# Turning h by DMA instead of on TensorE, and spreading the forward convolution over three blocks of the down product

## The chip, the cores and the metric

The kernel runs on one core of a Trainium2 chip. Its time is the device time of one execution in microseconds (us). In profiles the engines are called PE (TensorE, the matrix engine), PEld (its weight loads), DVE (VectorE), ACT (ScalarE), POOL (GpSimd) and SP (SyncE, which here only issues DMAs). A letter q behind an engine's name (SPq) means the engine's queue, where instructions wait and DMAs are issued.

## The reference

One call computes a small model's output and the gradients of all its inputs but one. S is 2048 rows, D is 1024, F is 3584; all tensors are bf16.

```
xn = layernorm(q)
kv = (4-tap shift convolution of k) * v
y  = causal convolution of kv with ssm_k over the rows (by FFT) + kv * ssm_D
s  = xn * y
h  = (xn @ w_gate) * (xn @ w_up)          # [S, F]
g  = silu(h @ w_down)                     # [S, D]
out = q + s * g
# outputs: out, then the gradients of sum(out * grad_out)
# by q, k, v, shift_k, ssm_k, ssm_D, w_gate, w_up, w_down
```

## The kernel before

The work runs in stages, each with its own matmuls on PE; the long convolution and its gradient run beside them, on DVE mostly.

1. **Start** (to 64 us): layer norm, transposes of xn (tiles `XNT`), tables for the Fourier transforms.
2. **Gate/up** (64 to 518 us): for 14 slabs `sl` of 256 columns of F and 16 row blocks, `gu_unit` multiplies four row blocks (a unit: 32 matmuls of 512 columns, line 645) with the slab `wslab`. ACT copies the products from PSUM to `gut` (647), DVE multiplies the two halves into `hN` (659), POOL stores `hN` to `Hd` (660) for the backward pass. The down product needs h with F on the partitions, so a function `turn` transposes each unit's eight 128x128 blocks on PE into PSUM (674); ACT copies them to `hT` (675); SP stores `hT` to the DRAM tensor `HTd` (666). `turn` is not called at once: `defer` puts it in a list, and `flush(5)` in each tick of a later unit calls the entries that are old enough.
3. **Down product, forward** (518 to 718 us): 16 blocks of 128 rows, 28 steps `fc` over F with two matmuls each (`bm_mm`, 969). The first two blocks run together in `bm_first`. `ht` tiles hold h turned, loaded from `HTd`; `WD` holds w_down, in seven loads. PSUM holds three blocks. Each finished block goes through `gate` (ACT: `bm`, `sig`, `sgn`; DVE: 11 multiplications and additions; POOL: four stores; SP: four loads, among them `yf_t`, the convolution's result, which `YFd` holds).
4. The gradients: dh and the gradients of w_gate and w_up (718 to 1335 us), of w_down (to 1523 us), of xn with the layer norm (to the end).

The **forward convolution** is a generator, `conv_forward`. For each of eight column blocks `ds` it transforms kv (`psF<-kv` on PE, ACT copies `SP`, sums on DVE into `W`, `KX`, `HX`), transforms the filter (`psF<-hx`), multiplies the spectra (`product`), and goes back (`inv_dft` on DVE, then `psY` on PE and `yf` on ACT, in `tail`). Every second `ds` computes the next kv (`shift`). `tick` pulls the generator: after `cnt` ticks it has to have done a share of its estimated work that `NT` sets. DVE's order is the order in which the operations are pulled (`PIN`, `keep_in_program_order`); the order on the other queues is a scheduler's. `drain` pulls what is left. In the kernel before, `bm_first` ticks 0.74 at every second step from step 5 on, and the generator is drained behind `bm_first`, before the gates of the first two blocks. At the end of the gate/up stage the flag `forward` is asserted to be down: the last `product` has begun, and the PSUM pool `ps_cv` of the transforms is given back.

Pools that matter here: `hN` has three buffers, `hT` two, `wslab` two, `ps_y` (PSUM of `psY`) one. The gates' pools (`mi`, `mt`, `mo`) take the room that the convolution's pools leave.

Of the kernel before, what the change touches and what calls it, by code (L numbers as in the profile page):

```python
# [19 lines left out]
def build_kernel(  # L20
# [11 lines left out]
    nc = tc.nc  # L32
# [579 lines left out]
    later = []  # L612
    gu_mm = [None]

    def defer(fn):
        later.append([0, fn])

    def flush(age=0):

# [8 lines left out]

    def gu_unit(sl, b0, n, w, tick):

        if n == 4:
            turn_of[0] += 1
            if turn_of[0] % 3 == 0 and sl < NSL - 2:
                gut = U[5][:, 2048:4096].rearrange("p (a i f) -> p a i f", a=2, i=4)
            else:
                gut = fg.tile([P, 2, 4, SLW], BF16, name="gut")
            hN = fg.tile([P, 2, 4, P], BF16, name="hN", bufs=3)
        else:
            gut = lnp.tile([P, 2, 2, SLW], BF16, name="gut_s", bufs=6)
            hN = lnp.tile([P, 2, 2, P], BF16, name="hN_s", bufs=6)  # L640
        for i in range(n):
            q, qi = divmod(b0 + i, 4)
            ps = ps_gu.tile([P, 512], F32, name="psg")
            for dc in range(DC):
                gu_mm[0] = nc.tensor.matmul(ps[:], XNT[q][:, dc, qi * P:(qi + 1) * P],  # L645
                                            w[:, dc].rearrange("p a f -> p (a f)"), start=(dc == 0), stop=(dc == DC - 1))
            nc.scalar.copy(out=gut[:, :, i], in_=ps[:].rearrange("p (a f) -> p a f", a=2))  # L647
            flush(5)
            if i == 0:
                turn_late()  # L650
            hn[0]()
            hn[0] = nop
            tick()
        sta(GUd[sl, b0 // 8][:, :, b0 % 8:b0 % 8 + n], gut[:, :, 0:n])

        def multiply():
            with tc.issue_after(last.ins) if b0 + n <= 4 and chunk[0] <= 2 else nullcontext():
                by_half = lambda t: t.rearrange("p i (a f) -> p a i f", a=2)
                tt(hN[:, :, 0:n], by_half(gut[:, 0, 0:n]), by_half(gut[:, 1, 0:n]), MUL)
            st(Hd[sl][:, :, b0:b0 + n, :], hN[:, :, 0:n])  # L660
            defer(turn)
        hn[0] = multiply

        def store(hT):
            fr, so = sl % 12 * SLW, b0 % 8 * P
            ld(HTd[b0 // 8][sl // 12][fr:fr + SLW, so:so + n * P].rearrange("(a f) s -> f a s", f=P),
               hT[:, :, 0:n].rearrange("f a i s -> f a (i s)"))

        def turn():
            hT = fg.tile([P, 2, 4, P], BF16, name="hT") if chunk[0] > 5 else lnp.tile([P, 2, 4, P], BF16, name="hT_s", bufs=5)  # L670
            ps = ps_tr.tile([P, 2, 4, P], BF16, name="tr")
            for a in range(2):
                for i in range(n):
                    nc.tensor.transpose(ps[:, a, i, :], hN[:, a, i, :], ident[:])
            nc.scalar.copy(out=hT[:, :, 0:n], in_=ps[:, :, 0:n])
            store(hT)
# [3 lines left out]
    INV8 = (2, 4, 6)  # L680
    SHIFT_W = 8 * 2.3

    conv_state = {"forward": True}

    def conv_forward():
        S_ = conv_state
# [83 lines left out]

        def transform(ds, kind, sp, X, C, ahead, step):

            if (ds, kind) in EIGHT:
                W = fwd4_buf(cs)[:].rearrange("p a b c x -> p (a b c) x")
                for n, w in enumerate(fwd8(sp, X, W, C, ahead)):
                    if n in (0, 2, 4, 6):
                        step()
                    yield net(w)
                return
            W = fwd4_buf(cs)  # L780
            fwd4_sums(W, sp[0], 0)
            step()
            yield net(2.4)
            fwd4_sums(W, sp[1], 1)
            step()
            yield net(2.4)
            fwd4_outs(X, W, 0)
            ahead(0)
            step()
            yield net(2.4)  # L790
            fwd4_outs(X, W, 1)
            ahead(1)
            step()
            yield net(2.4)
# [9 lines left out]
        for ds in range(8):  # L804
            yield 0.5
            if ds % 2 == 1 and ds < 7:
                with tc.issue_after(S_["kst"].ins):
                    for c in range(2):
                        load_kv(ds // 2 + 1, c)
            D0 = Dz[:, ds * P:(ds + 1) * P]  # L810
            sph = []
            KX = cx.tile([P, 16, 256], BF16, name="KX")
            HX = cs.tile([P, 16, 256], BF16, name="HX", bufs=2)
            own_room = lambda X: X[:].rearrange("p a x -> p (a x)").bitcast(F32).rearrange("p (a x) -> p a x", a=8)[:, 0:4]
            eight = (ds, 1) in EIGHT
            if ds == 0:
                yield from transform(0, 1, sp, HX, own_room(KX), lambda i: sph.append(half(0, kvs(0), i)), nop)
            else:
                yield from transform(ds, 0, sp, KX, own_room(HX), lambda i: sph.append(half(ds, S_["hx"], i, D0)), nop)
                S_["kst"] = st(KFd[ds], KX[:])  # L820
            next(tl, None)
            room = cf.tile([P, 4, 256], F32, name="room", tag="hx")[:] if eight else None
            yield from transform(ds, int(ds > 0), sph, HX if ds else KX, room, nop1 if eight else lambda c: h_rows(ds + 1, c),
                                 lambda: next(tl, None))
            if ds == 0:
                S_["kst"] = st(KFd[0], KX[:])
            if eight:
                h_rows(ds + 1, 0)
            turned(HX, 1, 0, 1)
            yield 1.3  # L830
            if eight:
                h_rows(ds + 1, 1)
            if ds == 7:
                cf.release()
                S_["forward"] = False
            st(HFd[ds], HX[:])
            yield from product(KX, HX, KX, cs, False, 0)
            if ds % 2 == 1 and ds < 7:
                yield from shift(ds // 2 + 1)
            sp = []  # L840

            def ahead():
                if ds < 7:
                    sp.append(half(ds + 1, kvs(ds + 1), len(sp)))
            yield from (inv8 if ds in INV8 else inv_dft)(KX, HX, cs, ahead if ds % 2 == 0 else None, ahead)
            if ds % 2 == 1:
                ahead()
            S_["G", ds] = HX
            tl = tail(ds)
# [61 lines left out]
    ps_cv = pool("ps_cv", 2, space=PSUM)  # L911
    pump, drain = make_pump(conv, F_TOTAL)
    cnt = [-5]
    NT = 24 * 8.0 + 14

    def tick(by=1):
        cnt[0] += by
# [55 lines left out]
    def bm_first(fcs):  # L973
        for fc in fcs:
            for i in range(2):
                mm = bm_mm(pss[i], lambda fc: HT0[fc // 16][:, fc % 16], i, fc)
            if fc % 2 == 1 and fc > 4:
                tick(0.74)
        return mm

    assert not conv_state["forward"]
    ps_cv.release()
    ps_bm = pool("ps_bm", 2, side="right", space=PSUM)
    pss = [ps_bm.tile([P, D], F32, name="psbm") for i in range(2)]
    with tc.issue_after(bm_first(range(4)).ins):
        flush()
    for p_ in (ps_gu, fg, fw):
        p_.release()

    ub = pool("ub", 1, side="right")
    U += [ub.tile([P, 4096], BF16, name=f"U{i}") for i in range(8, 12)]
    bw = pool("bw", 2, side="right")
    mh = [pool("mh0", 1, side="right")]
    ps_bx = pool("ps_bx", 1, space=PSUM)
# [181 lines left out]
    bpump, bdrain = make_pump(conv_backward(), C_TOTAL)  # L1179

    ddo = const.tile([P, 8], BF16, name="ddo")
    WD += [u8(j, a=4) for j in (2, 3, 9)]
    DBMT = [u8(q, a=DC) for q in (10, 8, 4, 5)]

    tr_name = ["tr"]
# [44 lines left out]
        return wdt  # L1230

    def load_ht(bp):
        if bp == 1:
            two_ = [u8(10, a=16), u8(8, a=16)]
            for f0, f1 in ((0, 16), (16, 24), (24, 28)):
                last = ld(two_[f0 // 16][:, f0 % 16:f0 % 16 + f1 - f0], ht_rows(bp, f0, f1))
            return (lambda fc: two_[fc // 16][:, fc % 16]), last
        ht = mh[bp % 2].tile([P, NF, 256], BF16, name="ht")
        for f0, f1 in ((0, 24), (24, 28)):
            last = ld(ht[:, f0:f1], ht_rows(bp, f0, f1))  # L1240
# [8 lines left out]
            ld(t, GUd[k // 2, k % 2])  # L1249
            DGU[k] = t  # L1250

    for j in range(4, 7):
        wd_ld = load_wd(j)
    with tc.issue_after(wd_ld.ins):
        ht1 = load_ht(1)
    with tc.issue_after(ht1[1].ins):
        ht2 = load_ht(2)
    bm_first(range(4, NF))
    drain()
    PIN[0] = False  # L1260
    mh.append(pool("mh1", 1, side="right"))
    mi = pool("mi", 2, side="right")
    mt = pool("mt", 1, side="right")
    mo = pool("mo", 2, side="right")
    for i in range(2):
        gate(i, pss[i])
    for bp in range(1, 8):
        ht, ht_ld = load_ht(bp) if bp > 2 else (ht1, ht2)[bp - 1]
        if bp in (3, 5, 7):
# [7 lines left out]
        for i in range(2):  # L1277
            ps = (ps_bx if (2 * bp + i) % 3 == 2 else ps_bm).tile([P, D], F32, name="psbm")
            for fc in range(NF):
                bm_mm(ps, ht, i, fc)  # L1280
                if fc == 18:
                    flush()
            gate(2 * bp + i, ps)
    for p_ in (ps_bx, ps_tr, ps_y, ps_bm, mo, mt, mi, mh[1], mh[0]):
        p_.release()
# [346 lines left out]
```

## Time and profile before

Median of three runs: 1928.6 us (1928.4 to 1930.85). The profiled execution took 1929.26 us; its span, from the first to the last instruction, is 1927.5 us. TensorE's granted clock was 1.00.

| stage (us) | PE busy | DVE busy | ACT busy | DMA share |
|---|---|---|---|---|
| 0 to 64 | 57.65 | 56.30 | 41.68 | 0.91 |
| 64 to 518 | 448.54 | 447.15 | 257.27 | 0.72 |
| 518 to 559 | 40.98 | 13.79 | 10.16 | 0.81 |
| 559 to 718 | 159.00 | 102.74 | 44.60 | 0.98 |
| 718 to 1335 | 616.88 | 547.65 | 185.38 | 0.74 |
| 1335 to 1523 | 188.00 | 143.07 | 40.21 | 0.86 |
| 1523 to 1927.5 | 400.88 | 231.84 | 59.35 | 0.87 |

The columns are busy time in us in each stretch; the DMA share is the mean busy share of the core's 16 DMA engines. A line such as `L674 PE MATMUL tr<-ident,hN 128*128 128x128 bf16 x416 | 31.9, 219 | 1.7 <-DVE hN L213 1.7` is a group of instructions: source line, engine, operation, what it writes from what, shape, count; then busy us in total and mean ns of one; then idle us of the engine just before them, and who ended it. DVE operations all have line 213, that of a helper, so they are told apart by their tiles. Matmuls overlap, so the time that one takes from PE's stream is read from the distance between starts: 0.216 us for 512 columns.

### The profile page before, as it was taken

The page shows a single profiled execution, that of the slowest core. Times are in us where ns is not written, and L with a number is a line of the kernel's source. Part 1 is how long each engine was busy: PE and PEld are TensorE (multiplying, and loading weights), DVE is VectorE, ACT ScalarE, POOL GpSimd, SP SyncE. Part 2 cuts the span into 40 slices and gives each one's busy share as a digit, 9 for nine tenths or more (in the row PEclk, how much of TensorE's full clock was granted, in tenths as well). Part 3 has the DMA queues.
Part 4 walks back from the last instruction along what each step waited for, and adds up shares of the span by engine and source line. Part 5 has one row for each costly group of instructions (what it writes and reads, how often), then busy time and mean ns, then how long its engine had stood idle before and what let it go on. Part 6 is the DMA issues. An engine that isn't in the chain of part 4 may idle for free.

```text
span 1927.5 us, 27456 instructions
## 1 busy us (share of the span) xinstructions
PE 1911.9 (99%) x10978; PEld 1030.1 (53%) x10978; DVE 1542.5 (80%) x1695; ACT 638.7 (33%) x943; POOL 331.0 (17%) x461
## 2 busy tenths in 40 slices
PE   8999999999999999999999999999999999999999
PEld 5555555555444456665666666664444444444444
DVE  8999999999937555888899999999996404287884
ACT  5854555555432233343222322222222102011113
POOL 5121212111112210000122131021211101011111
PEclk9999999999999999999999999999999999999999
DMA  9776866758899987666788698575786999889975
GB/s 297 264 259 221 257 211 229 234 197 266 270 278 312 298 291 257 209 201 218 264 243 264 234 247 263 201 262 186 224 253 174 143 205 217 168 178 188 189 180 171
DMA packets 451360, 444.43 MB, mean 231 GB/s; under 512 B 268800, under 2 KB 371612, under 8 KB 436768
## 3 DMA queue, kind: packets, MB, share of 16 engines
q1 hardware_dynamic: 394848, 243.36, 47.9%
q0 software_dynamic: 40064, 169.95, 27.6%
q10 hardware_dynamic: 16320, 29.36, 4.2%
q8 instruction: 86, 1.41, 0.3%
q14 instruction: 42, 0.34, 0.1%
HBM read 194.00 MB, written 185.64 MB: 197 GB/s over the span
## 4 chain that ended last, share of the span: by engine, by line
PE 80%; DVE 15%; issue 3%; DMA 1%; ACT 1%; SPq 0%; POOL 0%; DVEq 0%; ACTq 0%; POOLq 0%
PE psb L1340 20%; PE psx L1470 20%; PE psb L1323 10%; PE psbm L969 10%; PE psb L1418 9%; PE psg L645 6%; DVE W L213 4%; DVE KX L213 3%; DVE HX L213 2%; DVE m L213 2%; PE psF L235 1%; DVE U L213 1%; DVE hN L213 1%; PE psY L438 1%; PE psY L1116 1%
## 5 line engine op out<-in xcount | busy, mean ns | idle before, releaser
L645 PE MATMUL psg<-wslab,U 128*128 128x512 bf16 x1792 | 407.2, 379 | 2.5 <-DMA wslab<-in_B_w_gate_dram 1.6
L1340 PE MATMUL psb<-U,U 128*128 128x512 bf16 x1792 | 397.1, 379 | 0.0
L1470 PE MATMUL psx<-U,dgut 128*128 128x512 bf16 x1536 | 332.8, 379 | 0.0
L1470 PEld LDWEIGHTS <-dgut 128*128 128x128 bf16 x1792 | 175.3, 98 | 211.4
L1340 PEld LDWEIGHTS <-U 128*128 128x128 bf16 x1792 | 175.2, 98 | 198.0
L645 PEld LDWEIGHTS <-U 128*128 128x128 bf16 x1792 | 172.5, 98 | 187.7 <-issue 2.3
L1323 PE MATMUL psb<-wdt,U 128*128 128x256 bf16 x1792 | 205.6, 273 | 0.0
L1323 PEld LDWEIGHTS <-U 128*128 128x128 bf16 x1792 | 175.3, 98 | 29.2
L1418 PE MATMUL psb<-U,U 128*128 128x512 bf16 x816 | 177.1, 379 | 0.0
L213 DVE TENSOR_TENSOR W<-W 128x1024 f32<-128x1024 f32 (+1 forms) x174 | 171.6, 1003 | 3.7
L1345 ACT CAST wb<-psb 128x512 bf16<-128x512 f32 x112 | 65.6, 586 | 315.1 <-PE psb L1340 313.4
L969 PE MATMUL psbm<-U,ht 128*128 128x512 bf16 x672 | 145.7, 379 | 0.0
L1418 PEld LDWEIGHTS <-U 128*128 128x128 bf16 x896 | 87.5, 98 | 104.5
L647 ACT CAST gut<-psg 128x512 bf16<-128x512 f32 x156 | 91.6, 588 | 119.4 <-PE psg L645 118.9
L1502 ACT ACTIVATE dx_t<-dxn 128x1024 bf16<-128x1024 f32 x15 | 15.9, 1057 | 324.6 <-DVE dxn L213 324.6
L1168 DVE SCALAR_TENSOR_TENSOR dkp<-dkT,kT 128x1024 bf16<-128x1024 bf16 (+2 forms) x64 | 78.4, 1224 | 38.9 <-DMA dkT<-DKSHd 36.9
L969 PEld LDWEIGHTS <-ht 128*128 128x128 bf16 x672 | 65.6, 98 | 78.6
L213 DVE TENSOR_TENSOR U<-U,dht 128x2048 bf16<-128x2048 bf16 x56 | 68.3, 1221 | 46.8 <-ACT dht L1325 46.7
L1325 ACT CAST dht<-psb 128x512 bf16<-128x512 f32 x112 | 65.7, 587 | 116.3 <-PE psb L1323 116.3
L66 POOL DMA_DIRECT2D Hd<-hN x54 | 37.3, 691 | 297.5 <-DVE hN L213 295.0
L213 DVE TENSOR_TENSOR dxn<-psx,dxna_t 128x1024 f32<-128x1024 f32 x15 | 18.3, 1222 | 78.2 <-PE psx L1470 73.3
L1449 ACT CAST wbs<-psb 128x512 bf16<-128x512 f32 x51 | 29.9, 586 | 145.7 <-PE psb L1418 134.2
(237 smaller groups left out, 2452.0 us busy)
## 6 DMA issues: line engine op xcount, KB each, us to landing
U<-GUd SPq DMA_DIRECT2D x28, 1024.0 KB, 8.2
DGd<-U SPq DMA_DIRECT2D x28, 1024.0 KB, 5.8
GUd<-gut ACTq DMA_DIRECT2D x39, 512.0 KB, 5.7
out_dram<-wb SPq DMA_DIRECT2D x112, 128.0 KB, 4.0
U<-Hd SPq DMA_DIRECT2D x14, 1024.0 KB, 6.0
Hd<-hN POOLq DMA_DIRECT2D x54, 256.0 KB, 4.2
HTd<-hT SPq DMA_DIRECT2D x52, 256.0 KB, 4.1
ht<-HTd SPq DMA_DIRECT2D x6, 1536.0 KB, 10.1
```

The costliest lines, as they stand in the source:

```text
L66: ins = nc.gpsimd.dma_start(out=out, in_=in_)
L213: pinned(V.tensor_tensor(o, a, b, op))
L645: gu_mm[0] = nc.tensor.matmul(ps[:], XNT[q][:, dc, qi * P:(qi + 1) * P], w[:, dc].rearrange("p a f -> p (a f)"), start=(dc == 0), stop=(dc ...
L647: nc.scalar.copy(out=gut[:, :, i], in_=ps[:].rearrange("p (a f) -> p a f", a=2))
L969: mm = nc.tensor.matmul(ps[:, dh * 512:(dh + 1) * 512], ht(fc)[:, i * P:(i + 1) * P], WD[fc // 4][:, fc % 4, dh * 512:(dh + 1) * 512], sta ...
L1168: ins = V.scalar_tensor_tensor(prod[:].rearrange("p r d -> p (r d)")[:, lo:H], dkT[:, 0, lo:H], 1.0, kT[:, 0, 13 + m + lo:13 + m + H], op0 ...
L1323: nc.tensor.matmul(ps[:, x * SLW:(x + 1) * SLW], DBMT[2 * hf + g][:, dc, (b % 4) * P:(b % 4 + 1) * P], wdt[:, dc, :], start=(dc == 0), sto ...
L1325: nc.scalar.copy(out=dht[:, 2 * e:2 * e + 2].rearrange("p b f -> p (b f)"), in_=ps[:])
L1340: nc.tensor.matmul(ps[:], XN[b // 4][:, b % 4, dc * P:(dc + 1) * P], dgus[b // 8][:, :, b % 8], start=(b == 0), stop=(b == NB - 1))
L1345: nc.scalar.copy(out=wb[:, dc % 2].rearrange("p a f -> p (a f)"), in_=ps[:])
L1418: nc.tensor.matmul(ps, h[:, f, b, :], DBM[b // 4][:, b % 4, dh * 512:(dh + 1) * 512], start=(b == 0), stop=(b == NB - 1))
L1470: nc.tensor.matmul(ps[:, dh * 512:(dh + 1) * 512], t[n][:, f, i * P:(i + 1) * P], WGU[n][:, f, dh * 512:(dh + 1) * 512], start=(n == 0 and ...
```

## The change

From slab 2 on, h is turned by a DMA transpose on SP from `hN` to `hT`, both in SBUF, instead of eight transposes on PE and a copy on ACT. The deferred call is made sooner (it enters the list with age 3), and the store of `hT` is deferred by itself. The flag `forward` is lowered at the last forward transform (`ds` 7, kind 1) instead of behind it; a second flag, `filters`, falls when the pool `cf` is given back. `NT` grows from 206 to 224, so each tick pulls less. The list is flushed before the first steps of the down product. `bm_first` ticks a whole tick at every second step from the first; the third block (`bp` 1, `i` 0) ticks too; the generator is drained behind the third block, and the first two gates come there, before the third's own. The loads of the last three parts of `WD` and of `ht1` are written ahead of step 4 of `bm_first`.

```diff
-    def defer(fn):
-        later.append([0, fn])
+    def defer(fn, age=0):
+        later.append([age, fn])
...
     def gu_unit(sl, b0, n, w, tick):
+        by_dma = n == 4 and sl >= 2 and chunk[0] > 5 and True
...
-            defer(turn)
+            defer(turn_dma if by_dma else turn, 3 if by_dma else 0)
...
+        def turn_dma():
+            hT = fg.tile([P, 2, 4, P], BF16, name="hT")
+            nc.sync.dma_start_transpose(out=hT[:].rearrange("p a i s -> p (a i) s"),
+                                        in_=hN[:].rearrange("p a i f -> p (a i f)"))
+            defer(lambda: store(hT), 2)
...
-    conv_state = {"forward": True}
+    conv_state = {"forward": True, "filters": True}
...
         def transform(ds, kind, sp, X, C, ahead, step):
+            if ds == 7 and kind == 1:
+                S_["forward"] = False
...
                 cf.release()
-                S_["forward"] = False
+                S_["filters"] = False
...
-    NT = 24 * 8.0 + 14
+    NT = 24 * 8.0 + 32
...
     def bm_first(fcs):
...
-            if fc % 2 == 1 and fc > 4:
-                tick(0.74)
+            if fc % 2 == 1:
+                tick()
...
-    with tc.issue_after(bm_first(range(4)).ins):
-        flush()
+    flush()
+    bm_first(range(4))
     for p_ in (ps_gu, fg, fw):
         p_.release()
     ub = pool("ub", 1, side="right")
     U += [ub.tile([P, 4096], BF16, name=f"U{i}") for i in range(8, 12)]
+    WD += [u8(j, a=4) for j in (2, 3, 9)]
+    for j in range(4, 7):
+        wd_ld = load_wd(j)
+    def load_ht1():
+        two_ = [u8(10, a=16), u8(8, a=16)]
+        for f0, f1 in ((0, 16), (16, 24), (24, 28)):
+            last = ld(two_[f0 // 16][:, f0 % 16:f0 % 16 + f1 - f0], ht_rows(1, f0, f1))
+        return (lambda fc: two_[fc // 16][:, fc % 16]), last
+    with tc.issue_after(wd_ld.ins):
+        ht1 = load_ht1()
+    fc_ = 4
+    while conv_state["filters"]:
+        bm_first([fc_])
+        fc_ += 1
     bw = pool("bw", 2, side="right")
...
-    for j in range(4, 7):
-        wd_ld = load_wd(j)
-    with tc.issue_after(wd_ld.ins):
-        ht1 = load_ht(1)
     with tc.issue_after(ht1[1].ins):
         ht2 = load_ht(2)
-    bm_first(range(4, NF))
-    drain()
-    PIN[0] = False
-    mh.append(pool("mh1", 1, side="right"))
-    mi = pool("mi", 2, side="right")
-    mt = pool("mt", 1, side="right")
-    mo = pool("mo", 2, side="right")
-    for i in range(2):
-        gate(i, pss[i])
+    bm_first(range(fc_, NF))
+    def gates_open():
+        drain()
+        PIN[0] = False
+        mh.append(pool("mh1", 1, side="right"))
+        out = [pool(*a, side="right") for a in (("mi", 2), ("mt", 1), ("mo", 2))]
+        return out
     for bp in range(1, 8):
...
                 bm_mm(ps, ht, i, fc)
                 if fc == 18:
                     flush()
+                if bp == 1 and i == 0 and fc % 4 == 3:
+                    tick()
+            if bp == 1 and i == 0:
+                mi, mt, mo = gates_open()
+                for j in range(2):
+                    gate(j, pss[j])
             gate(2 * bp + i, ps)
```

More of the change, by code (lines that the diff above doesn't have):

```diff
@@ L1181, in build_kernel @@
     ddo = const.tile([P, 8], BF16, name="ddo")
-    WD += [u8(j, a=4) for j in (2, 3, 9)]
     DBMT = [u8(q, a=DC) for q in (10, 8, 4, 5)]
@@ L1232, in load_ht @@
     def load_ht(bp):
[L1233 to L1237, printed above, removed]
         ht = mh[bp % 2].tile([P, NF, 256], BF16, name="ht")
```

## The prediction, made before the changed kernel ran

> **What bounds the kernel now.** I read the page's busy times first, then the stages, then the waits inside the stage that the change touches, then the few rows that price its pieces.
>
> ```profile
> PE 1911.9 (99%) x10978; PEld 1030.1 (53%) x10978; DVE 1542.5 (80%) x1695; ACT 638.7 (33%) x943; POOL 331.0 (17%) x461
> ...
> PE 80%; DVE 15%; issue 3%; DMA 1%; ACT 1%; SPq 0%; POOL 0%; DVEq 0%; ACTq 0%; POOLq 0%
> ```
>
> PE (TensorE) is the bound, but the chain that ended last runs 15% through DVE (VectorE). The busy time by stage says where:
>
> ```profile
> core 0: us, PE busy (x) PEld busy (x) DVE busy (x) ACT busy (x) POOL busy (x), PEclk, DMA share, GB/s
> ...
> 64.00:518.00 454.00, 448.54 (x2789) 250.09 (x2788) 447.15 (x412) 257.27 (x363) 76.33 (x108) 1.00 0.72 237
> 518.00:559.00 41.00, 40.98 (x218) 20.56 (x217) 13.79 (x13) 10.16 (x12) 1.84 (x2) 1.00 0.81 233
> 559.00:718.00 159.00, 159.00 (x757) 72.91 (x756) 102.74 (x164) 44.60 (x45) 38.11 (x60) 1.00 0.98 303
> ```
>
> In the gate/up stage (64 to 518) PE and DVE are both at 98 to 99%: two engines with equal work, each pacing the other. In the next 41 us, the down product's first three blocks, DVE has 13.8 us of work, and in the 159 us after that 102.7. So PE work taken out of 64 to 518 is worth something only if DVE work leaves that stage too, and the place with room for it is 518 to 559. The change does both. The clock is 1.00 everywhere.
>
> **Part 1: 48 PE turns removed.** A turn is eight 128x128 transposes. In the trace in order of time (PE, around 304) the pitch is read from the starts:
>
> ```profile
> 303.81 0.61 PE L674 MATMUL tr<-ident,hN 128*128 128x128 bf16 x8
> 304.25 1.91 PE L235 MATMUL psF<-kv,TF 128*128 128x256 bf16 x16
> ```
>
> 0.44 us a turn (the 0.61 overlaps what follows). Twelve slabs by four units: 48 x 0.44 = 21.1 us of PE's stream. The waits before these turns go too, and so, I think, do those before the first transforms of each kv pair. The groups of PE in 64 to 530 show them (last column, idle before):
>
> ```profile
> L674 PE MATMUL tr<-ident,hN 128*128 128x128 bf16 x416 | 31.9, 219 | 1.7 <-DVE hN L213 1.7
> L235 PE MATMUL psF<-kv,TF 128*128 128x256 bf16 x224 | 27.4, 272 | 3.2 <-DVE kv L213 3.1
> ```
>
> The second goes because of the pacing: I summed the rows along both queues of the built program up to where PE first reads the second, third and fourth kv. PE's sum is ahead of DVE's by 3.1, 5.9 and 8.2 us in the kernel before and by 6.7, 10.6 and 15.6 in the changed one: DVE has 4 to 7 us more to be ready in. So PE: -21.1 - 1.7 - 3.2 = -26.0. ACT loses 48 copies of 1.02 us; at 57% busy it bounds nothing, so I count nothing.
>
> **Part 2: 48 DMA turns added.** On SP's queue each unit now has a DMA transpose, then the store of hT, which waits for the transpose to land. For a DMA transpose of the same 256 KB there is one row, from HBM:
>
> ```profile
> dgut<-DGd SPq DMA_TRANSPOSE x168, 4.2
> ```
>
> 4.2 us from issue to landing (2.6 to 20.2 in the tile's own view), 1.22 us of SP's queue. Of the rate: in 1540 to 1600 nearly nothing but transposes runs, at 207 GB/s with the DMA engines full, so 262 KB take 1.27 us of all sixteen. 48 x 1.27 = 61 us spread over some 420: DMA share 0.72 to about 0.87. No operation of the stage waits long for a DMA (KX for the KFd store, 0.7 us in all), and the loads for the convolution stand ahead of their use (k issued at 317, read at 391), so I count nothing; without that cover each late load costs its lateness on DVE. A source in SBUF is not in the trace: I take the HBM row, since it moves the same blocks; bounds are 2.6 and 20.2.
>
> SP's queue per unit: 4.2 + 0.36 = 4.6 us of 8.5 us (PE's time per unit after the change, about 409 us by 48). Behind a waiting store stand the next transpose and the slab loads; a slab is loaded a slab ahead (some 34 us), so nobody waits.
>
> **Part 3: the convolution's end.** DVE's work up to its last operation is the same set of instructions. It ends in the trace here:
>
> ```profile
> 527.06 2.36 DVE L213 TENSOR_TENSOR HX<-W 128x1024 bf16<-128x1024 f32 x2
> ```
>
> that is 529.4. DVE is 99% busy up to there, so I leave this time where it is. Only the place of PE moves: before, PE came to the last four inverse products (psY) at 541.96, 12.5 us after DVE; now PE has them behind the third block.
>
> There the four groups stand in a row with one PSUM buffer, each waiting for ACT's copy of the one before, and the fourth block's PSUM is freed by the first gate's bm copy, behind the last yf copy on ACT. The prices are here:
>
> ```profile
> 548.03 1.04 PE L449 MATMUL psY<-HX,TI 128*128 128x256 bf16 x8
> ...
> 549.10 0.59 ACT L749 CAST yf<-psY 128x512 bf16<-128x512 f32 x1 [1.15 <-PE psY L449]
> ...
> 549.59 1.02 ACT L1200 CAST bm<-psbm 128x1024 bf16<-128x1024 f32 x1
> ```
>
> A group to its copy 1.07, copy 0.59, handover 0.1: a pitch of 1.76 instead of 0.87, three times: 2.7. After the fourth: 1.07 + 0.49 + 1.02 + 0.1 = 2.7 less its own 0.87: 1.8. A new wait of 4.5 us on PE, where before there was none (those copies lay beside the third block).
>
> **Sum, made at the start of the fourth block**, since behind it PE's queue is the same in both. Before: 518.4 + 168 matmuls x 0.216 + two turns 0.9 + four psY groups 3.5 = 559.1. After, along PE: 559.1 - 26.0 + 4.5 = 537.6. After, along DVE: 529.4 + 0.1 + 3 x 1.76 + 2.7 = 537.5. Two chains that meet within 0.1 us rarely both hit; I add 0.5, so the gain is 21. The profiled execution took 1929.26 (span 1927.5), 0.7 over the median of 1928.6: 1908.3 by its own time, 1907.6 by the median. I say 1908.
>
> **What moved behind, and its cover.** The first two gates (22 DVE operations, eight loads on SP, eight stores on POOL) start about 9 us later against PE. In the trace bm copies of gates 0 to 3 start at 549.6, 554.0, 564.9, 575.1; with gate 0 one us ahead of the fourth block, the fifth, sixth and seventh block get their PSUM at 4.3, 15.2 and 25.5 us after its start and need it at 12.1, 24.2 and 36.3. DVE catches up in the 56 us that it has free in 559 to 718. On SP the loads of ht for the seventh block stand behind yf_t of gate 1, which waits for the last YFd store (last yf copy to the first read of yf_t: 9.4 us); they are needed 36 us on. All covered; if not, PE pays one for one. The DMA engines are 98% busy there, so that cover is thinner than the sum says.
>
> **Rivals.**
> *Late loads at the seam.* The last unit's h is ready on DVE around 493; transpose +4.2, store +4.1, then on SP the last w_down load, landing at about 509, and 1 MB of ht (12.2 in its row) at about 515. PE needs them at 511 and 514. DVE's 529.4 hides about 2 us more. For: the DMA queues are full there and landings reach 20.2. Against: medians fit. A landing of 10 instead of 4.2 costs some 5, one of 20.2 about 15: 1913 to 1923.
>
> *SP serialised, slower.* SP takes transpose, store, transpose in order, and the store waits for the landing L. If L + 0.36 is over 8.5 us for the whole stage, SP falls behind, the three hN buffers fill, DVE stops at the next h, and with it PE. Each unit then costs L + 0.36 - 8.5; 21 us are eaten at L = 8.6. At L = 10.1, half the longest landing seen, 48 x 1.96 = 94 and the kernel takes 2002. For: no transpose from SBUF in the trace. Against: 168 from HBM at 4.2, on engines that were fuller; one of 1 MB (U<-DBMd) landed in 7.1.
> The Trainium skill speaks for this rival: its page "VectorE: DVE Perf Modes", section "The three transpose paths", gives a 128x128 block 390 ns on TensorE and 1309 ns by DMA, and its rules say to use TensorE where the output may be PSUM. By that, eight blocks one after another would be an estimated 10.5 us, and the kernel about 2020. The trace disagrees with both figures where it has them: 55 ns a block in PE's stream, and eight blocks from HBM landed in 4.2 us.
>
> *Better than the sum.* DVE's 4.7 idle us of 100 to 520 vanish as well (ACT freer): 1903.
>
> **How the numbers follow.** Forecast (both chains hold within 5 us, 1904 to 1913) 0.65; late loads (1913 to 1926) 0.14; better 0.06; SP serialised 0.12; 0.03 in between, within 0.2% of 1928.6 (3.9 us, about what a measurement of this kernel can tell from no change). Faster 0.85, same 0.03, slower 0.12. The range 1902 to 1926 leaves out the slower rival, the same, and the best end.
>
> **What would show it.** Right: no L674 from slab 2 on; L674's and kv's waits gone; last HX write near 529; PE's psY groups at a pitch of 1.8 and a first gap before the fourth block, near 538; transposes landing in 4 to 6 us; rows behind shifted by 21. Wrong: hN waiting for a DMA, psbm waiting for U<-in_B_w_down or U<-HTd, the last HX write later than 533, or DVE's gates late enough for a psbm to wait on bm after the fourth block.

## The result, and the profile after

The changed kernel took 1949.84 us (median; 1943.3 to 1955.16) beside 1929.59 for the kernel before: a ratio of 1.0103 (95% interval 1.008 to 1.0126), 1.0% slower. 1908 was forecast. The profiled execution took 1946.05 (span 1944.2), 16.8 over that of before. One execution of a later kernel, e7 (1988.1 us), was slow, and its median leaves it out.

The page's busy times and chain, then the stages (us, busy time and instructions of PE, PEld, DVE, ACT, POOL, clock, DMA share, GB/s):

```profile
PE 1902.7 (98%) x10594; PEld 1011.8 (52%) x10594; DVE 1542.3 (79%) x1695; ACT 594.0 (31%) x895; POOL 330.7 (17%) x461
...
PE 62%; ACT 0%; issue 0%; DVE 0%; ACTq 0%
```
```profile
64.00:518.00 454.00, 436.38 (x2438) 232.47 (x2437) 424.41 (x387) 214.47 (x317) 75.13 (x107) 0.98 0.95 259
518.00:559.00 41.00, 30.30 (x123) 12.92 (x122) 34.46 (x34) 1.17 (x2) 1.70 (x2) 0.83 1.00 245
559.00:718.00 159.00, 155.35 (x740) 71.62 (x738) 96.85 (x154) 47.32 (x49) 36.47 (x57) 0.99 0.98 274
```

The chain's shares end at 62%, so it is read no further. In 64 to 518 PE and DVE are no longer full (17.6 and 29.6 us idle instead of 5.5 and 6.9), and the clock is no longer 1.00. In 518 to 559 DVE has work, as intended, but PE stands for 10.7 us. The DMA share went from 0.72 to 0.95, where 0.87 was forecast.

The turns are gone from PE's groups (64 to 530), with the waits for hN and kv; others have come:

```profile
L646 PE MATMUL psg<-wslab,U 128*128 128x512 bf16 x1600 | 361.4, 382 | 11.1 <-ACT gut L648 6.1 <-ACT U L648 4.9
L235 PE MATMUL psF<-kv,TF 128*128 128x256 bf16 x224 | 29.0, 283 | 6.3 <-ACT SP L257 6.3
```

PE waits for copies on ACT, which is busy 47% of that stage. What holds ACT is in the trace in order of time around 131 us, SP's queue first, then ACT's queue and ACT, then PE:

```profile
110.05 2.53 SPq L672 DMA_TRANSPOSE hT<-hN  x1
131.05 0.36 SPq L61 DMA_DIRECT2D HTd<-hT  x1
```
```profile
131.10 0.52 ACTq L72 DMA_DIRECT2D GUd<-gut  x1
131.74 0.58 ACT L648 CAST U<-psg 128x512 bf16<-128x512 f32 x1 [9.34 <-DMA hT<-hN]
```
```profile
133.29 3.57 PE L235 MATMUL psF<-kv,TF 128*128 128x256 bf16 x16 [6.32 <-ACT SP L257]
```

The transposition issued at 110.05 landed 21.0 us later. ACT reads no hT, and yet its copy is put down to that landing: in ACT's queue the store of gut to GUd stands ahead of the copy, and it uses the same completion counter as the transposition. PE then stands for 6.32 us. In the view of the tile hT, landings (stores of hT included) run from 2.1 over a median of 4.4 to 24.2 us. The 48 transpositions alone have a median of 5.4 (64 to 545), and 11 of them took over 10 us. With the queues otherwise nearly empty one takes 3.1:

```profile
hT<-hN SPq DMA_TRANSPOSE x48, 5.4
```

The packets by queue, first in such a quiet stretch (253.3 to 256.5), then in those 21 us (110 to 131); q1 carries SP's DMAs, q10 ACT's, q0 POOL's; packets, MB, share of the 16 engines:

```profile
q1 hardware_dynamic: 1328, 0.52, 71.2%
q10 hardware_dynamic: 111, 0.19, 15.9%
```
```profile
q0 software_dynamic: 888, 3.44, 58.5%
q10 hardware_dynamic: 523, 1.02, 28.3%
q1 hardware_dynamic: 1328, 0.52, 19.4%
```

Each q1 row holds two DMAs, the transposition and the store of hT that was issued just ahead of it. What a transposition has by itself follows from q1 over the whole execution, before and then after:

```profile
q1 hardware_dynamic: 394848, 243.36, 47.9%
```
```profile
q1 hardware_dynamic: 445536, 255.95, 53.3%
```

50,688 packets more for 48 transpositions are 1056 each, for 256 KB. (So 1328 packets, here and in the expectation of e5 below, are 1056 and the store's 272.) While the 1328 went, 1411 packets of the other two queues went too, POOL's at 3.9 KB each (loads of k and v, stores of hN). That is near one for one: it looks as if the engines take the queues in turn, packet by packet, so that something cut into many small packets waits for as many large ones. The clearest stretch is 461 to 463, where POOL stores KX in packets of 8 KB and SP loads `ht` in packets of 512 bytes, and no other queue has work:

```profile
q0 software_dynamic: 97, 0.79, 94.0%
q1 hardware_dynamic: 97, 0.05, 8.2%
```

Packets go one for one, bytes sixteen for one. The Trainium skill, page "DMA: Bandwidth & Descriptors", section "Queues, rings and completion order", says that each engine goes round the queues by packets; these counts agree.

A transposition stood behind that load on SP's own queue. SP took 13.81 us to issue it (the longest in the view of hT, min/median/max in ns), and it landed after 19.2 us:

```profile
L672 SPq DMA_TRANSPOSE hT<-hN x48: 1237/1630/13807, 96.8 to 528.1; - x48
```

So lateness comes from two sides: from what goes ahead on SP's own queue, and from what the other queues send meanwhile.

At the seam, where the down product follows the gate/up stage, PE in order of time:

```profile
535.62 5.30 PE L978 MATMUL psbm<-U,U 128*128 128x512 bf16 x16 [3.41 <-DMA U<-in_B_w_down_dram]
548.21 18.14 PE L978 MATMUL psbm<-U,U 128*128 128x512 bf16 x72 [7.29 <-DMA U<-in_B_w_down_dram]
566.18 1.04 PE L449 MATMUL psY<-HX,TI 128*128 128x256 bf16 x8
567.94 1.03 PE L449 MATMUL psY<-HX,TI 128*128 128x256 bf16 x8 [0.72 <-ACT yf L756]
569.64 1.03 PE L449 MATMUL psY<-HX,TI 128*128 128x256 bf16 x8 [0.67 <-ACT yf L756]
571.35 1.03 PE L449 MATMUL psY<-HX,TI 128*128 128x256 bf16 x8 [0.67 <-ACT yf L756]
573.97 2.29 PE L978 MATMUL psbm<-U,U 128*128 128x512 bf16 x5 [1.59 <-ACT bm L1220]
```

The fourth block starts at 573.97 instead of 559.1 (forecast: 537.6). DVE's last write of HX, at 529.4 before, ends at 552.9:

```profile
550.58 2.36 DVE L213 TENSOR_TENSOR HX<-W 128x1024 bf16<-128x1024 f32 x2
```

### The profile page after: what moved, and what is told of

Read it like the earlier page. It is cut to its first block, busy times and chain, and to the rows that moved or that the text cites. A ratio compares the mean times of both kernels' runs of the same rounds, so it can differ in the third digit from the quotient of the medians.

```text
span 1944.2 us, 26676 instructions
## 1 busy us (share of the span) xinstructions
PE 1902.7 (98%) x10594; PEld 1011.8 (52%) x10594; DVE 1542.3 (79%) x1695; ACT 594.0 (31%) x895; POOL 330.7 (17%) x461
## 4 chain that ended last, share of the span: by engine, by line
PE 62%; ACT 0%; issue 0%; DVE 0%; ACTq 0%
PE psb L1356 20%; PE psx L1486 20%; PE psb L1339 10%; PE psb L1434 9%; PE psY L1137 1%; PE psY L438 1%; PE psx L1434 1%; PE psF L235 1%; PE psbm L978 0%; PE psY L1434 0%; ACT B L295 0%; DVE dbm L213 0%; PE tr L1242 0%; ACT wbs L1581 0%; ACT wb L1361 0%
## 5 line engine op out<-in xcount | busy, mean ns | idle before, releaser
L213 DVE TENSOR_TENSOR W<-SP 128x1024 f32<-128x1024 f32 x64 | 74.5, 1221 | 6.0 <-ACT SP L257 3.0
```

What stands on the lines that cost most here:

```text
L213: pinned(V.tensor_tensor(o, a, b, op))
```

## The experiments

Medians in us; ratios to the kernel before (1928.9 to 1929.6 beside each) with 95% intervals. The views show one execution of each kernel: in e1, e11 and e12 that was the slowest one, in e8 the second fastest (1924.95).

| kernel | turns by DMA | first gates | median | ratio |
|---|---|---|---|---|
| changed | 48 | behind block 3 | 1949.8 | 1.0103 (1.008 to 1.0126) |
| e1 pacing alone | 0 | behind | 1945.7 | 1.0093 (1.0063 to 1.0124) |
| e2 turns alone | 48 | in front | 1941.8 | 1.0076 (1.0047 to 1.0105) |
| e3 GUd off ACT | 48 | behind | 1955.4 | 1.0138 (1.0114 to 1.0163) |
| e4 seam on PE | 40 | behind | 1949.0 | 1.0094 (1.0062 to 1.0125) |
| e5 plain copies | 48 copies | behind | 1915.6 | 0.9929 (0.9907 to 0.9952) |
| e6 loads spread | 48 | behind | 1964.3 | 1.0169 (1.0119 to 1.0218) |
| e7 spread, seam on PE | 40 | behind | 1961.1 | 1.0166 (1.0122 to 1.021) |
| e8 quiet units | 24 | behind | 1933.8 | 1.0018 (1.0002 to 1.0034) |
| e9 no DMA, old pace | 0 | behind | 1942.9 | 1.0064 (1.0047 to 1.0081) |
| e11 gates in front | 0 | in front | 1931.9 | 1.0017 (1.0008 to 1.0026) |
| e10 quiet, old gates | 24 | in front | **1919.3** | 0.9953 (0.994 to 0.9967) |
| e12 burst units | 24 others | in front | 1935.8 | 1.0022 (0.9998 to 1.0046) |

**e1 and e2: each half alone.**

```diff
e1, from the changed kernel:
-        by_dma = n == 4 and sl >= 2 and chunk[0] > 5 and True
+        by_dma = False
e2, from the kernel before: only turn_dma, by_dma and the two deferrals are added
```

> The changed kernel with all of h turned on PE again (by_dma is False): the new pacing, gates and load order without one DMA turn. Theory A (the 48 DMA turns cost the time): without them the loss of 20 us goes. PE has its 21.1 us of turns back, DVE's work is spread over 518 to 574 as in the changed kernel; the new wait of 4.3 us before the fourth block stays, kv's 3.2 us of waits go: 1927 to 1934, no stall over 2 us on PE before the fourth block. Theory B (the pacing costs it: DVE's convolution ends too late, the blocks behind wait): the loss stays and the turns come on top of it: 1955 to 1971.

> The kernel before with only the 48 DMA turns: old pacing, old gates, old order of loads. Theory A (the DMA turns cost the time): PE loses 21.1 us of turns, but DVE stays at 98% of the gate/up stage, so little of that is gained, and the stalls that the turns bring (26 us in 64 to 500, some 14 at the seam) come whole: 1945 to 1970. Theory B (the turns are free, the pacing costs): DVE bounds the stage as before, 1922 to 1930.

Each half alone is slower: 1945.7 and 1941.8. e2 came nearer theory A, 3 us below its range. For e1 theory A failed: without one DMA turn 17 us are lost, and theory B's range was missed as well. The waits of PE in 500 to 1300 say where:

```profile
PE tr L1242 <- DVE dbm L213: 12.8, 2, 7.2
PE psY L449 <- ACT yf L756: 2.1, 3, 0.7
PE psbm L978 <- ACT bm L1220: 1.6, 1, 1.6
```

At the end of the down product PE waits for the gates' products (dbm). In e1 the slower pace meets a PE that still has its turns, so the convolution's last HX write ends at 557.5 and the gates come late. So late turns are not the only thing that can cost such a kernel its time.

**e3: the store to GUd off ACT's queue.**

```diff
     def sta(out, in_):
-        return nc.scalar.dma_start(out=out, in_=in_)
+        return nc.gpsimd.dma_start(out=out, in_=in_)
```

> The changed kernel with the stores of gut to GUd issued on POOL instead of ACT; the turns stay on DMA. Theory C (the loss inside the gate/up stage is ACT: its store to GUd shares a completion counter with a late transposition, waits for it, and the copies of gut behind it are late): of the 38 us that stalls and the lower clock cost, the 26 of 64 to 500 shrink to under 8, no copy on ACT waits for DMA hT<-hN, and the time falls to 1925 to 1935. Theory D (the DMA engines are full, the turns land late and hold hN, hT or SP themselves): ACT's waits change their name, the stalls stay over 18 us and the time 1944 to 1955.

Slower still: 1955.4. ACT no longer waits for any transposition, as theory C had it, and the waits moved, as theory D had it, 0.4 us above its range (waits in 64 to 518):

```profile
DVE hN L213 <- DMA hT<-hN: 21.7, 4, 13.2
PE psg L646 <- DMA wslab<-in_B_w_gate_dram: 9.7, 2, 5.9
```

Behind a late transposition, SP holds the slab loads and hN stays taken. ACT's queue was only the first way in which lateness reached PE.

**e4: the seam's eight turns on PE.**

```diff
+        by_dma = n == 4 and 2 <= sl < NSL - 2 and chunk[0] > 5
```

> The changed kernel with the turns of the last two slabs (8 of 48 units) on PE again; 40 stay on DMA. Theory E (the seam: late last transpositions stand ahead of the loads of w_down on SP, and PE waits for those, 10.7 us, and runs at a clock of 0.83 behind it): the two waits psbm<-U<-w_down go, the eight turns cost 8 x 0.44 = 3.5: 1934 to 1940. Theory F (DVE's convolution, whose last HX write came at 552.9, sets the fourth block, whatever the loads do): PE only waits elsewhere, at psY or bm, and the time stays 1946 to 1953.

Theory F's time, and half of its mechanism. The waits for w_down went, and the fourth block started at 563.81, 10.2 us sooner, so the loads had held it; the median did not move. PE waits for dbm at the end of the down product instead: 9.4 us, where the changed kernel had 0.3.

**e5: plain copies in place of transpositions.**

```diff
-            nc.sync.dma_start_transpose(out=hT[:].rearrange("p a i s -> p (a i) s"),
-                                        in_=hN[:].rearrange("p a i f -> p (a i f)"))
+            nc.sync.dma_start(out=hT[:].rearrange("p a i s -> p (a i s)"),
+                              in_=hN[:].rearrange("p a i f -> p (a i f)"))
```

> The changed kernel with each of the 48 DMA transpositions replaced by a plain DMA copy of the same 256 KB from hN to hT, in the same place on SP (it leaves out the transposition, so what depends on h turned is not computed). Queue, order, waits, bytes and pacing stay; a transposition is 1328 packets in the trace, the copy some 128 to 260. Theory G (the 16 DMA engines serve the queues packet by packet; in the bursts of POOL's loads and stores, of 4 KB a packet, a transposition's many small packets each wait for a large one): the copies land in under 8 us in the bursts too, the 26 us of stalls in 64 to 500 fall under 6, the last HX write comes before 535: 1905 to 1920. Theory H (256 KB more on a full set of engines, or SP's order, is enough): landings over 10 us in the bursts stay, and so do over 15 us of stalls: 1938 to 1955.

1915.6, in theory G's range. The same bytes go in the same place on the same queue, but a copy has 144 packets instead of 1056 (q1 has 401,760 over the execution), lands after 2.3 us in a quiet stretch, and is issued in a median of 0.47 us instead of 1.63. PE's first psbm starts at 491.25 (513.45 in the changed kernel, 518.44 before), and the last HX write ends at 532.0. The first psbm before, and then with copies:

```profile
518.44 3.62 PE L969 MATMUL psbm<-U,U 128*128 128x512 bf16 x16
```
```profile
491.25 1.03 PE L978 MATMUL psbm<-U,U 128*128 128x512 bf16 x4
```

PE's waits in 64 to 1300 are small:

```profile
PE psY L449 <- ACT yf L756: 2.5, 5, 0.7
PE psbm L978 <- DMA U<-HTd: 2.2, 1, 2.2
PE psbm L978 <- ACT bm L1220: 1.6, 1, 1.6
```

One point of the expectation failed: four copies still landed after more than 10 us (the longest 17.0), one of them in the first burst (14.2). So the form of the transposition is the cost, and bytes, queue and order are not; that it works through the packets' turns is the reading of the counts above, not shown apart from the longer issue and the engine time (by the trace's packet records, in quiet, 1.4 us of all 16 engines for a transposition, 0.7 for a copy).

**e6 and e7: the loads of k and v spread out**, alone and with the seam's turns on PE.

```diff
-            if ds % 2 == 1 and ds < 7:
-                with tc.issue_after(S_["kst"].ins):
-                    for c in range(2):
-                        load_kv(ds // 2 + 1, c)
+            # k of the next kv: two pieces in the even block; v: two in the odd one
```

> The changed kernel with the loads of k and v for the next kv taken apart: instead of 2.4 MB at the start of every odd column block, k in two pieces in the even block before and v in two pieces in the odd one. All bytes and all 48 transpositions stay. Theory G (bursts on POOL's queue starve the transpositions packet by packet): in 64 to 500 the longest landing falls from 24 us to under 13, the stalls from 26 us to 5 to 12, the last HX write from 553 to under 540: 1918 to 1935, what is left being the seam. Theory I (the engines are too full on the whole, DMA share 0.95): the same queue time in other places, stalls over 20 us: 1942 to 1955.

> The spread loads, and the turns of the last two slabs on PE. If the stage's stalls made DVE late and that hid what the seam's repair was worth, both repairs add up now: no wait for w_down, the last HX write near 535, no wait of the gradient's transposes for dbm at the end of the down product: 1910 to 1922, below the kernel before. If the DMA engines' load as such is the bound, 1938 to 1952.

Both missed: 1964.3 and 1961.1. The longest landings stayed (25.7 and 25.1): the 1 MB stores of KX and HX were still there, and the pieces of k now stood beside them. Five landings (e6) and six (e7) took over 15 us instead of four; why the loss of e6 grew by 14 us is not settled.

**e8 and e9: half of the turns, and none, with the gates behind the third block.** e8 sends 24 units by DMA, away from the bursts and the seam (21 of their transpositions had landed within 10 us in the changed kernel, the other three after 10.9, 11.2 and 19.2; of the other 24 units, eight had taken over 10); both pull the last four psY groups inside the third block.

```diff
e8:
+    BY_DMA = (0, *range(4, 12), 16, *range(20, 25), *range(28, 36), 39)
+            by_dma = dma_unit[0] in BY_DMA
-    NT = 24 * 8.0 + 32
+    NT = 24 * 8.0 + 20
+                    if fc in (11, 15, 19, 23):
+                        next(conv, None)
e9: by_dma = False, NT = 24 * 8.0 + 14, the same two last lines
```

> 24 of the 48 turns by DMA, those whose transpositions landed early in the changed kernel (away from the bursts of POOL's queue and from the seam), the other 24 on PE; NT 212 instead of 224, since PE loses only half of the turns; the last four psY groups are pulled at steps 11, 15, 19 and 23 of the third block instead of behind it. Theory G (a late transposition stalls, an early one is free): 24 x 0.44 = 10.6 us leave PE without stalls over 3 us, the 4.3 us before the fourth block go: 1912 to 1920. If the DMA engines' load as such costs, half of the turns cost half of it: landings over 12 us appear in new places and the time is 1930 to 1945.

> No turn by DMA, NT 206 as in the kernel before, the gates behind the third block and psY in it, as in the run of 24 turns. It is the floor for that run: what order and pacing do without one DMA turn. With the pace back, DVE's convolution ends near 530 as in the kernel before, so nothing should be late at the end of the down product: 1926 to 1931. If it is the new order of gates and loads that costs (and not the pace of the run with the new pacing alone, whose DVE ended at 557), it stays at 1938 to 1950.

In e8 the gate/up stage did what was wanted (first psbm at 508.7, 9.7 us earlier, no wait over 3 us), yet the median is 1933.8, in the range that was given for the load as such; one landing over 12 us (13.0) is little for that theory. e9 points to another cost. There DVE's last HX write ends at 531.5, near the 529.4 of the kernel before, and 14 us are lost all the same. The waits on SP's queue (500 to 740), and one window of the kernel before, then of e9:

```profile
SPq L61 <- PE psY L449: 18.0, 1, 18.0
```
```profile
540.00:560.00 20.00, 20.00 (x110) 10.64 (x109) 3.46 (x6) 7.64 (x10) 1.15 (x1) 1.00 0.82 215
```
```profile
540.00:560.00 20.00, 20.00 (x107) 10.18 (x105) 0.00 (x0) 1.64 (x3) 0.00 (x0) 1.00 0.46 110
```

The gates' tiles take the convolution's room, so their loads wait for the last psY: the first x_t is loaded at 562.1 instead of 549.1. Until then the DMA engines stand half idle (0.46 instead of 0.82), and in 600 to 718 they were full already in the kernel before (0.97), so it looks as if the lost time does not come back: yf_t comes late, DVE waits for it 26.7 us (6.6 before), and PE waits 5.0 for dbm. This account is not complete: in e5 the engines stand as idle (0.43 in 521 to 542), x_t is loaded as late against PE (539.96, the fourth block at 541.51), and PE never waits for dbm.

**e10 and e11: the gates in front of the third block again.** e10 is the kernel before with e8's 24 units by DMA; e11 is e9 with the gates moved.

```diff
e10, from the kernel before: turn_dma, by_dma by BY_DMA, and
-    NT = 24 * 8.0 + 14
+    NT = 24 * 8.0 + 20
-            if fc % 2 == 1 and fc > 4:
-                tick(0.74)
+            if fc % 2 == 1:
+                tick()
e11: gates_open() and the two gates ahead of "for bp in range(1, 8)"
```

> The kernel before with 24 of the 48 turns by DMA (the same quiet units as in the run of 24 turns), NT 212 and whole ticks in the first two blocks, and everything else as before: the convolution drained and the first two gates opened in front of the third block. Theory J (two costs: late transpositions in the bursts, and gates opened behind the third block, whose loads come too late for a stage in which the DMA engines are full): both are gone, PE loses 24 x 0.44 = 10.6 us, the gates' first load is issued at 537 to 541 instead of 549, and the time is 1916 to 1923, below the kernel before. If the gain of the quiet turns is eaten by the stage behind whatever the gates do: 1927 to 1935, with waits of PE for ht or dbm.

> As the run without DMA turns at the old pace (1942.9), but the convolution is drained and the first two gates are opened in front of the third block; flags, order of loads and whole ticks stay as changed. Theory J (the place of the gates costs those 14 us: their loads start at 562 instead of 549 and the DMA engines stand half idle at 540 to 560): 1927 to 1931. If the changed order of the loads of w_down and ht costs it: 1938 to 1945.

Theory J in e10, with 1919.3, below both kernels; e11's 1931.9 is 0.9 above its range. From e11 to e9 only the place of the gates differs, and with it that of the drain and of the last psY groups: 10.9 us. The other 2.9 of e11 over the kernel before go with what else it takes from the changed kernel (order of loads, flags, ticks). In e10 the first x_t is loaded at 539.9, 9.2 us earlier than before, PE's first psbm starts at 508.36, and the stages are full again:

```profile
64.00:518.00 454.00, 445.77 (x2605) 244.44 (x2652) 448.23 (x414) 238.03 (x342) 76.62 (x109) 1.00 0.85 257
518.00:559.00 41.00, 40.79 (x204) 20.15 (x206) 22.09 (x27) 12.02 (x14) 4.30 (x6) 1.00 0.88 243
559.00:718.00 159.00, 158.26 (x793) 77.40 (x805) 101.10 (x159) 46.78 (x49) 37.35 (x60) 1.00 1.00 311
```

**e12: the same number of turns, the other units.**

```diff
-            by_dma = dma_unit[0] in BY_DMA
+            by_dma = dma_unit[0] not in BY_DMA
```

> The same kernel as the last one with 24 turns (1919.3), with the choice turned round: the other 24 units go by DMA, the 16 in the bursts of POOL's queue and the 8 at the seam, and the quiet ones stay on PE. Number of turns, bytes, pace and gates are the same. Theory G (where a transposition falls decides): the stalls of the kernel with all 48 come back nearly whole: 1934 to 1946. If the number of transpositions decides (load of the DMA engines as a whole): 1917 to 1924.

1935.8, in theory G's range: 16.5 us between two kernels that differ only in which 24 units go by DMA. Eight of the 24 transpositions took over 10 us, the longest 23.9; in e10 it was one. The waits of PE (64 to 560) are of the changed kernel's kind:

```profile
PE psg L651 <- ACT gut L653: 14.3, 1, 14.3
PE psbm L981 <- DMA U<-in_B_w_down_dram: 6.6, 2, 3.8
PE psF L235 <- ACT SP L257: 5.3, 3, 4.1
```

## Why the prediction was wrong

**Part 1 held.** In e10, 24 turns fewer end the gate/up stage 10.1 us sooner: 0.42 each, 0.44 forecast. The waits for hN and kv went in the changed kernel, as said. With copies in the place of the transpositions (e5) the down product starts at 491.25; 492.4 was forecast.

**Part 2 is the step that failed**, at "I take the HBM row, since it moves the same blocks", then "I count nothing" and "nobody waits". The median was near (4.2 forecast, 5.4 measured), and so were the bounds (2.6 to 20.2; 3.1 to 24.2). But the sum used the median, and one landing of 21 us is enough to hold SP, ACT and PE. The same holds for SP's queue: 1.22 us an issue were forecast, and one took up to 13.8. The rate came from a stretch with almost nothing but transposes (1540 to 1600), where those of the row landed within 5.2 us; the 20.2 of the same row lay elsewhere, and what made it was not asked. The price of the engines was right in quiet (1.27 us of all sixteen forecast, 1.4 by the packet records) and short under load: the DMA share rose to 0.95 instead of 0.87, and (0.95 - 0.72) x 454 / 48 is 2.2 us a turn, an estimate that holds what the other queues' packets took longer. The gate/up stage should have ended at 492.4 and ended at 513.45. Of these 21 us, 17.4 are the new waits of the two groups above; I put the rest down to the clock, 0.97 in 64 to 200 behind the first long wait.

**The rival "SP serialised"** had the right sign and the wrong mechanism: it asked for a landing over 8.6 us through the whole stage. SP did wait for landings (195.9 us, 46 times, longest 18.5, in 64 to 518), but the turns of quiet stretches cost next to nothing (in e10 one of 24 landed after 16.1 us, ahead of PE's one wait over 2 us, 2.9), and the loss came by single landings. By the page "VectorE: DVE Perf Modes" of the Trainium skill, section "The three transpose paths", the loss would have been an estimated 91 us. Its advice to use TensorE is borne out in the bursts and at the seam (e12) and not in the quiet units (e10), and its figure of 1309 ns a block is not: eight blocks took 3.1 us in quiet and 24.2 at most.

**The rival "Late loads at the seam"** was real: 10.7 us of waits for w_down behind transpositions that landed after 13.3 and 12.2 us. It was not enough by itself: e4 removes them and gains nothing.

**Part 3** had its new wait right: a pitch of 1.70 to 1.76 and 4.3 us in all (7.79 from the first psY to the fourth block, less 4 x 0.87), 4.5 forecast. DVE's end at 529.4 held where nothing stalled (532.0 with copies) and not in the changed kernel (552.9): DVE stands where PE and ACT stand.

**"All covered"** held in the changed kernel and failed in its neighbours. Behind the fourth block PE waits 0.3 us for dbm in the changed kernel and not at all in e5, but 12.8 in e1, 9.4 in e4 and 5.0 in e9, and from e11 to e9 the place of the gates costs 10.9 us. The gates were priced on DVE and SP; the DMA engines, "98% busy there", were named and not priced. Why the cover holds in e5 and not in e4, where x_t is loaded as far ahead of the fourth block (1.6 us), stays open. Of the 16.8 us of the changed kernel's profiled execution, 14.9 were lost ahead: its fourth block starts at 573.97 instead of 559.1.

**What e5 leaves of the 21 us.** Its fourth block starts at 541.51, 3.9 us later than the forecast 537.6; 2.9 of that are waits for w_down and `ht` at the seam. Another 1.9 are lost from there to the end of the down product, where the clock was 0.91 in 540 to 560. That leaves the 15.7 us that its profiled execution gained (1929.26 to 1913.59); the median gained 13.8.

## What to carry to other kernels

A transfer that replaces engine work is priced with what else its queues carry at that moment, not by the median of a quiet stretch; what counts is the longest landing and who stands behind it on every queue that shares its completion. When each repair only moves the wait to another engine (ACT, then SP, then DVE), take the cause away at the source: here the transpositions that fall into bursts. And where the DMA engines are full in the stage behind, the start of its first loads can be worth as much as PE's time (e9 and e11), though not in every kernel here.

## What was not expected of the hardware

- A plain copy of 256 KB within SBUF is 144 packets and landed in 2.3 us, a transposition of the same bytes 1056 packets and 3.1 us. The Trainium skill, page "Advanced Engine Details and Errata", section "X-Bar Transpose (TRN2)", calls the two equally fast; here they are not, and under load far from it (1915.6 against 1949.8 us for the kernel).
- A transposition on SP's queue held ACT for 9.34 us through ACT's own store, which touches none of its data.
- Two queues shared the engines by packets and not by bytes: 97 packets each in two us, 0.79 MB of the one and 0.05 of the other.
- Kernels with late landings or late gates repeat badly: 1937.7 to 1957.2 for e1, 1926.6 to 1947.8 for e12, beside 1919.1 to 1922.6 for e10 and 1928.1 to 1930.1 for the kernel before, run beside e10 (beside e12 two of 13 of its executions took 1934.6 and 1941.5).
